# Splitting the query projection between two layers into two halves, and a new order of the kept heads

## The chip, the cores and the metric

The kernel runs on one core of a Trainium2 chip. The metric is the device time of one launch in microseconds (us). Three runs of the kernel before took 1135.45, 1135.97 and 1137.13 us, so the median is 1135.97 us. TensorE is called PE here (its weight loads PEld), VectorE DVE, ScalarE ACT, GpSimd POOL, and SyncE, which issues every transfer, SP.

## The reference, cut to what matters

Two identical layers follow each other. Each is an attention block over a key/value cache and then a small mixer MLP. There are 8 batch elements with one token each, 16 query heads on 8 key/value heads, 4096 cached positions, 256 numbers to a head, and a model width of 448.

```
q = (x @ wq).reshape(B, Sq, Hq, Dh)            # 448 x 4096
scores = einsum(q, k) * Dh ** -0.5             # k, v: 8 x 8 x 4096 x 256 each
p = softmax(scores);  o = einsum(p, v)
x = x + o.reshape(B, Sq, Hq * Dh) @ wo         # 4096 x 448
x = x + mixer(x)                               # layernorm, w1..w4, gelu
# and the same again with the same caches and weights
```

With one token the shifts of the mixer bring in zeros only, so its first half reduces to `x1 = x`, and what is left is a layernorm, `w3`, gelu and `w4`. Both layers read the same caches. The second layer needs a batch element's keys and values again, with a query that is known only when that element has gone through the first layer and its MLP.

## The kernel before, in words

**Units.** The work is a list of units, written out by hand around line 354. A unit (p, b, g) is layer p (1 or 2), batch element b, key/value head g. A unit has four steps, each with one tile of keys and one tile of values of 128 x 2048 bf16 numbers (512 KB). For a batch element come first the units of layer 1, then `GAP, lone..., GAP`, then the units of layer 2. A GAP is an empty unit. A lone unit belongs to another batch element; it gives the engines something to do while this element's attention output goes through `wo`, the MLP (`mid_steps`) and `wq`. Batch elements 0 to 3 have two lone units there, elements 4 to 7 one. This text calls the stretch from the last layer-1 unit to the first layer-2 unit of the element the passage, and the place where the layer-2 units begin the fence (the dict `fence`, line 372).

**Kept and loose heads.** Keys arrive raw, DVE transposes them (line 502), and `k_part` (line 590) multiplies them with the block-diagonal query `Qblk`. Heads 2 to 7 (`KEEP` = 6) keep their transposed keys in SBUF from layer 1 to layer 2, apart from two tiles that are parked in PSUM and copied back by ACT (line 474). Heads 0 and 1 are loose: their keys are loaded and transposed a second time. Values are always loaded twice (`v_part`, line 569).

**Slots.** There are 31 slots of 512 KB. Of those, 22 hold kept keys during a passage, so that everything else goes round in the other nine. `pump` (line 465) takes the next transfer of a fixed list and the slot that came free longest ago. SP issues the transfers in that order, one behind the other; each waits until the last reader of its slot is done, and at most eight are under way.

**Order of the values.** `plan` says at which step a value tile is used: six steps after its keys' step as a rule, earlier for the last head of layer 1. `late_v` makes an exception: the two loose layer-2 heads of the element before are scored between the kept heads of layer 2, but their values are held back to the next passage (these are the held heads; their probabilities lie in `pt_far`). Their eight value tiles were planned at steps 0, 1, 4, 5, 6, 7, 8 and 9 of the passage, the last head's own at steps 2, 2, 3 and 3.

**The dense steps.** `mid_steps` (line 256) is a generator. The main loop takes one piece of it per step through `dense_next`; what the pieces leave for DVE and ACT waits in `between` and is emitted at the next `flush`. Its last pieces are `variance` and the query projection: 16 groups of seven matmuls with `wq` (`in_mms`, lines 132 and 140), then one ACT multiplication `scaled` (line 340) that writes the query. When that is emitted, `make_blocks` may call `expand` for the first layer-2 units (PE line 155, ACT line 161). At the fence the loop runs whatever is left of the generator (line 735) before the first `k_part` of layer 2.

**PE is in order.** A matmul whose tile has not landed holds up all that follows on PE, the dense steps too.

Of the kernel before, what the change touches and what calls it, by code (L numbers as in the profile page):

```python
# [18 lines left out]
KEEP = 6  # L19
# [8 lines left out]
def kernel(  # L28
# [14 lines left out]
    nc = tc.nc  # L43

    Bn, Sq, D = A_x.shape
    G, S, Dh = A_k_cache.shape[1:]
# [4 lines left out]
    HJ = Hq * 2  # L51
# [16 lines left out]
    nr, xm, cc, hx, hu = (  # L68
        small[:, 21:23],
        small[:, 23:27],  # L70
        small[:, 27:31],
        small[:, 31:45],
        small[:, 45:59],
    )
# [3 lines left out]
    wq_sb = consts.tile([128, 3, HD], BF16, name="wq_sb")  # L78
    wq_tl = consts.tile([128, HD // 2], BF16, name="wq_tl")
# [110 lines left out]
    between = []  # L190

    def flush():
        while between:
            between.pop(0)()

    q_done = set()
# [54 lines left out]
    def bursts(n, k, spread):  # L251

        m = -(-n // k) if spread else n
        return [range(i, min(i + m, n)) for i in range(0, n, m)]

    def mid_steps(b, spread):

        xs = X[:, b, :]  # L260
        res = {}

        def first():
            nc.vector.tensor_tensor(out=xs, in0=xs, in1=y1[:, b, :], op=ALU.add)
            total(xs)

        between.append(first)
        yield
        norm_rows(xs, res)
        yield  # L270
        variance(TWICE)
        hT = work.tile([128, HC], BF16, tag="hT", bufs=1)
        hpf = room(HC)
        hp = hpf.rearrange("p (i m) -> p i m", i=2)
        for ms in bursts(HC // 2, 2, spread):
            in_mms(hp[:, :, ms[0] : ms[-1] + 1].unsqueeze(3), w3_sb, w3_tl, res["rows"], HC, ms)
            if ms[-1] + 1 < HC // 2:
                yield

        def gelu():  # L280
            nc.vector.tensor_scalar(
                out=hx, in0=hpf, scalar1=nr[:, 1:2], scalar2=None, op0=ALU.mult
            )
            nc.vector.scalar_tensor_tensor(
                out=hu, in0=hx, scalar=0.044715, in1=hx, op0=ALU.mult, op1=ALU.mult
            )
            nc.vector.scalar_tensor_tensor(
                out=hu, in0=hu, scalar=1.0, in1=hx, op0=ALU.add, op1=ALU.mult
            )
            nc.scalar.activation(hu, hu, ACT.Tanh, scale=0.7978845608028654)  # L290
            nc.vector.scalar_tensor_tensor(
                out=xs, in0=cc, scalar=nr[:, 0:1], in1=xs, op0=ALU.mult, op1=ALU.add
            )

            between.append(
                lambda: nc.vector.scalar_tensor_tensor(
                    out=hT[:], in0=hu, scalar=1.0, in1=hx, op0=ALU.add, op1=ALU.mult
                )
            )

        between.append(gelu)
        yield
        yield
        yp = room(4)
        for cs in bursts(4, 2, spread):
            for c in cs:
                for m in range(HC):
                    nc.tensor.matmul(  # L308
                        yp[:, c : c + 1],
                        chunk(w4_sb[:, m, :], c),  # L310
                        hT[:, m : m + 1],
                        start=(m == 0),
                        stop=(m == HC - 1),
                    )
            if cs[-1] < 3:
                yield

        def more():
            nc.vector.scalar_tensor_tensor(
                out=xs, in0=yp, scalar=0.5, in1=xs, op0=ALU.mult, op1=ALU.add  # L320
            )
            total(xs)

        between.append(more)
        yield
        norm_rows(xs, res)
        yield

        variance(((256.0, 256.0 * EPS),))
        q2 = qT2[:, :, b % 2].rearrange("p (i m) -> p i m", i=2)  # L330
        qp = room(HJ).rearrange("p (i m) -> p i m", i=2)
        for ms in bursts(HJ // 2, 3 if spread else 2, True):
            in_mms(
                qp[:, :, ms[0] : ms[-1] + 1].unsqueeze(3), wq_sb, wq_tl, res["rows"], HJ, ms, True
            )
            if ms[-1] + 1 < HJ // 2:
                yield

        def scaled():
            nc.scalar.mul(q2, qp, nr[:, 0:1])  # L340
            q_done.add(b)

        between.append(scaled)

    heads = list(range(G))
    loose = heads[: G - KEEP]

    second = heads[G - KEEP // 2 :] + heads[G - KEEP : G - KEEP // 2]  # L350
    parked = {(second[-1], 4 - PARKED + i): i for i in range(PARKED)}
    GAP = None
    ahead = {b: [(2, b - 1, g) for g in loose] for b in range(1, Bn)}
# [3 lines left out]
    units = []  # L357
    ends = {}
    fence = {}
    late_v = {}  # L360
    half = KEEP // 2
    for b in range(Bn):
        if b:
            units += [(1, b, g) for g in heads[len(loose) :]]
        else:
            units += [(1, b, g) for g in heads[:-half]] + ahead[0] + [(1, b, g) for g in heads[-half:]]
        ends[len(units) - 1] = b
        at = 4 * len(units)
        ps = [(units.index(u), s) for u in ahead[b] for s in range(4)]
        late_v.update(zip(ps, [at + i for i in (0, 1, 4, 5, 6, 7, 8, 9)]))  # L370
        units += [GAP] + lone[b] + [GAP]
        fence[len(units)] = b
        units += [(2, b, g) for g in second[:half]] + ahead.get(b + 1, []) + [(2, b, g) for g in second[half:]]
# [13 lines left out]
    t = 0  # L387
# [127 lines left out]
    def dense_next():  # L515
        flush()
        if dense and next(dense[0], "end") == "end":
            dense.pop(0)
# [3 lines left out]
    def make_blocks(t):  # L522

        if t in runs and t not in ready:
            p, b, g = units[t]
            if p == 1 or b in q_done:
                x, n = runs[t]
                qT = qT1[:, :, b] if p == 1 else qT2[:, :, b % 2]
                expand(Qblk[x], qT[:, 4 * g : 4 * (g + n)], n, scb[t % 2])
                ready.add(t)  # L530
# [49 lines left out]
    def k_part(t, s):  # L580
        u = units[t]
        p, b, g = u
        if s == 0:
            scs[t] = scb[t % 2][:, 0:64].rearrange("p (c b h) -> p c b h", b=4, h=2)
        key = (u if fresh(u, s) else (1, b, g)), s
        ktv = kt_of[key][:].rearrange("p (e c m x) -> p e c m x", e=4, c=2, x=2)
        for c in range(2):
            for db in range(4):
                for x in range(2):
                    nc.tensor.matmul(  # L590
                        scs[t][:, 2 * s + c, :, :],
                        ktv[:, db, c, :, x],
                        Qblk[run_of[t][0]][:, run_of[t][1], db, x, :, :],
                        start=(db == 0 and x == 0),
                        stop=(db == 3 and x == 1),
                    )
        if p == 2 or g in loose or (g, s) in parked:
            free.append(kt_of.pop(key))
            pump()
# [129 lines left out]
    for t in range(n_units + 1):  # L729
        cur = t < n_units  # L730
        for q in range(4):
            i = 4 * t + q
            if cur:
                if t in fence and q == 0:
                    while dense:
                        dense_next()
                    flush()
                    make_blocks(t)
                late = q == 0 and t and not beside[t]
                if beside[t]:  # L740
                    transposes(i)
                flush()
                if not late and not beside[t]:
                    transposes(i)
                if units[t]:
                    k_part(t, q)
            back = t and units[t - 1]
            if q == 0 and back:
                max_mms(t - 1)
                exps(t - 1)  # L750
            if cur and late:
                transposes(i)
            if back and q == 1:
                to_rows(t - 1)
                sums(t - 1)
            if q == 2 and not cur:
                mark(t - 2)
            for u, s in plan.get(i, []):
                v_part(u, s)
                if s == 3:  # L760
                    head_out(u)
            if q == 3 and cur and t > 1 and t - 2 not in ends:
                mark(t - 2)
            if q == 3 and t - 1 in ends:
                mark(t - 1)
            dense_next()
            if q > 1:
                make_blocks(t + 1)
            if cur and units[t] and q == 3:
                max_reduce(t)  # L770
# [112 lines left out]
```

## Time and profile before

The profiled execution took 1135.04 us, of which its span is 1133.0 us; that is 0.93 us under the median of the three runs.

| what | value |
|---|---|
| span | 1133.0 us |
| DMA moved | 449.83 MB, mean 397 GB/s |
| PE busy / PEld busy | 62% / 57% of the span |
| DVE / ACT / POOL busy | 49% / 27% / 9% |
| chain that ended last: transfers | 66% |
| transfers of 512 KB | 512 of values, 320 of keys |
| median from issue to landing | 9.9 us |

The page's second part cuts the span in 40 equal slices of 28.3 us and gives the busy tenths of each engine and the rate of the transfers in each. The chain of part 4 is followed back from the last instruction to whatever released each step. "Issue" in it is time in which an engine waited for nothing that the profile shows. Further views used are a table of busy times by stretch, the timeline of a stretch, and the list of what SP waited for.

### The profile page before, as it was taken

The page shows a single profiled execution, that of the slowest core. Times are in us where ns is not written, and L with a number is a line of the kernel's source. Part 1 is how long each engine was busy: PE and PEld are TensorE (multiplying, and loading weights), DVE is VectorE, ACT ScalarE, POOL GpSimd, SP SyncE. Part 2 cuts the span into 40 slices and gives each one's busy share as a digit, 9 for nine tenths or more (in the row PEclk, how much of TensorE's full clock was granted, in tenths as well). Part 3 has the DMA queues.
Part 4 walks back from the last instruction along what each step waited for, and adds up shares of the span by engine and source line. Part 5 has one row for each costly group of instructions (what it writes and reads, how often), then busy time and mean ns, then how long its engine had stood idle before and what let it go on. Part 6 is the DMA issues. An engine that isn't in the chain of part 4 may idle for free.

```text
span 1133.0 us, 47063 instructions
## 1 busy us (share of the span) xinstructions
PE 700.0 (62%) x20769; PEld 641.9 (57%) x20769; DVE 554.9 (49%) x1305; ACT 308.1 (27%) x1384; POOL 104.4 (9%) x156
## 2 busy tenths in 40 slices
PE   3155666666766576665666666655666666665765
PEld 3144565555655466555655556655656565655665
DVE  5267445544464445643556434643456435643332
ACT  2022124221342213321243212422143213421241
POOL 0000001000010000100010000000010000100001
DMA  9999999999999999999999999999999999999991
GB/s 361 386 417 418 413 391 415 417 416 399 416 416 417 407 392 413 417 417 400 406 415 417 417 396 358 417 416 417 363 400 417 416 411 372 416 417 417 372 415 77
DMA packets 127196, 449.83 MB, mean 397 GB/s; under 512 B 13568, under 2 KB 19600, under 8 KB 126608
## 3 DMA queue, kind: packets, MB, share of 16 engines
q1 hardware_dynamic: 126992, 446.83, 98.5%
q8 instruction: 162, 2.65, 0.8%
q14 instruction: 42, 0.34, 0.1%
HBM read 446.77 MB, written 0.01 MB: 394 GB/s over the span
## 4 chain that ended last, share of the span: by engine, by line
DMA 66%; PE 16%; DVE 6%; issue 5%; ACT 4%; SPq 2%; POOL 0%; POOLq 0%; DVEq 0%; ACTq 0%
DMA slot<-in_A_v_cache_dram 43%; DMA slot<-in_A_k_cache_dram 22%; PE bank L569 5%; DVE slot L502 4%; PE bank L590 3%; PE bank L132 2%; SPq L478 2%; ACT pt L657 1%; PE bank L613 1%; PE bank L177 1%; DVE small L623 1%; ACT pe L626 1%; PE bank L308 1%; PE bank L649 1%; ACT slot L474 1%
## 5 line engine op out<-in xcount | busy, mean ns | idle before, releaser
L502 DVE STREAM_TRANSPOSE slot<-slot 128x512 f32<-128x512 f32 x640 | 414.6, 688 | 215.9 <-DMA slot<-in_A_k_cache_dram 142.4
L569 PEld LDWEIGHTS <-slot 128*128 128x128 bf16 x8192 | 268.9, 105 | 335.0 <-DMA slot<-in_A_v_cache_dram 300.8
L569 PE MATMUL bank<-pt,slot 128*128 128x2 bf16 x7168 | 260.8, 166 | 269.0 <-DMA slot<-in_A_v_cache_dram 237.4
L590 PE MATMUL bank<-Qblk,slot 128*128 128x8 bf16 x8192 | 294.4, 168 | 41.6 <-issue 19.5
L590 PEld LDWEIGHTS <-slot 128*128 128x128 bf16 x8192 | 266.6, 105 | 49.0 <-issue 33.2
L626 ACT ACTIVATE pe<-bank,small 128x32 bf16<-128x32 f32 x256 | 61.7, 297 | 435.1 <-DVE small L623 435.0
L668 POOL TENSOR_TENSOR small<-small 128x2 f32<-128x2 f32 x112 | 78.4, 700 | 779.6 <-DVE small L664 779.6
L657 ACT CAST pt<-bank 32x64 bf16<-32x64 f32 x448 | 91.1, 203 | 108.1 <-PE bank L649 103.7
L623 DVE TENSOR_REDUCE small<-bank 128x2 f32<-128x256 f32 x128 | 54.1, 422 | 116.4 <-PE bank L613 116.1
L664 DVE TENSOR_REDUCE small<-bank 128x2 f32<-128x64 f32 x128 | 28.1, 220 | 141.4 <-ACT pt L657 91.3
L161 ACT CAST Qblk<-bank 32x32 bf16<-32x32 f32 (+1 forms) x304 | 53.0, 174 | 81.8 <-PE bank L155 78.0
L613 PE MATMUL bank<-rows,small 128*128 128x128 bf16 x256 | 48.6, 293 | 18.9 <-DVE small L605 18.8
L569 PE MATMUL bank<-pt_far,slot 128*128 128x2 bf16 x1024 | 37.6, 166 | 25.1 <-DMA slot<-in_A_v_cache_dram 22.6
L649 PE MATMUL bank<-pe,rows 128*128 128x64 bf16 x512 | 51.3, 241 | 1.9 <-issue 1.9
L649 PEld LDWEIGHTS <-rows 128*128 128x128 bf16 x512 | 33.8, 124 | 29.3 <-issue 29.3
L639 PE MATMUL bank<-pe,small 128*128 128x64 bf16 x128 | 27.3, 213 | 28.8 <-ACT pe L626 27.6
L605 DVE TENSOR_REDUCE small<-bank 128x2 bf16<-128x64 f32 x128 | 25.5, 199 | 35.4 <-PE bank L590 35.0
L177 PEld LDWEIGHTS <-wo_sb 128*128 128x128 bf16 x1152 | 35.4, 104 | 7.3 <-issue 7.3
L538 ACT ACTIVATE OT<-bank,small 128x2 bf16<-128x2 f32 x122 | 25.6, 261 | 48.0 <-PE bank L569 47.2
L132 PEld LDWEIGHTS <-wq_sb 128*128 128x128 bf16 x864 | 30.1, 106 | 13.2 <-issue 8.7
L474 ACT COPY slot<-park 128x1024 bf16<-128x1024 bf16 x32 | 31.0, 1027 | 23.7 <-DVE slot L502 23.7
L177 PE MATMUL bank<-OT,wo_sb 128*128 128x1 bf16 x1024 | 33.1, 165 | 4.5 <-ACT OT L538 4.5
(113 smaller groups left out, 386.6 us busy)
## 6 DMA issues: line engine op xcount, KB each, us to landing
slot<-in_A_v_cache_dram SPq DMA_DIRECT2D x512, 512.0 KB, 9.9
slot<-in_A_k_cache_dram SPq DMA_DIRECT2D x320, 512.0 KB, 9.9
wo_sb<-in_A_wo_dram SPq DMA_DIRECT2D x4, 896.0 KB, 9.2
wq_sb<-in_A_wq_dram SPq DMA_DIRECT2D x3, 1024.0 KB, 6.9
w_sb<-in_B_w_dram SPq DMA_DIRECT2D x1, 1568.0 KB
w_sb<-in_B_w_dram SPq DMA_DIRECT2D x3, 448.0 KB, 10.1
wq_tl<-in_A_wq_dram SPq DMA_DIRECT2D x2, 256.0 KB, 10.1
w_tl<-in_B_w_dram SPq DMA_DIRECT2D x2, 112.0 KB, 9.3
```

The source lines that it names most:

```text
L132: nc.tensor.matmul(pv[:, i, j, :], cols(big[:, c, :], m + i * half), rows[:, c, :], start=(i == 0 and j == 0 and c == 0), stop=True, skip_ ...
L161: nc.scalar.copy(dst, src)
L177: nc.tensor.matmul(y[:, c, :], chunk(wo_sb[:, k, :], c), o[:, k, :], start=False, stop=True, skip_group_check=True,)
L502: nc.vector.transpose(dst[:, q], src[:, q])
L569: nc.tensor.matmul(pos[t][:, k, :], vv[:, c, 128 * k : 128 * k + 128], pts[t][:, 8 * s + c, :], start=(t == 0 and s == 0 and c == 0 and k ...
L590: nc.tensor.matmul(scs[t][:, 2 * s + c, :, :], ktv[:, db, c, :, x], Qblk[run_of[t][0]][:, run_of[t][1], db, x, :, :], start=(db == 0 and x ...
L613: nc.tensor.matmul(mzs[t][:, 128 * h : 128 * h + 128], pm[:, h : h + 1].to_broadcast([128, 128]), ident, start=True, stop=True,)
L623: nc.vector.tensor_reduce(nm, mx, AX.X, ALU.max, negate=True)
L626: nc.scalar.activation(pe[:].rearrange("p c b h -> p h (c b)")[:, h], scs[t].rearrange("p c b h -> p h (c b)")[:, h], ACT.Exp, bias=nm[:, ...
L649: nc.tensor.matmul(pp[:, c], sel, pe[:], start=True, stop=True)
L657: nc.scalar.copy(pts[t][sl].rearrange("p (k c) h -> p k c h", c=4), pp[sl, :, :, pb, :].rearrange("p c k h -> p k c h"),)
L668: nc.gpsimd.tensor_tensor(out=rz_of[t], in0=zs, in1=mone, op=ALU.pow)
```

## The change

1. The 16 groups of the query projection are cut in two. Part 1 (groups 8 to 15: heads 2, 3, 6 and 7) comes first, with its own `scaled`; then the generator passes two steps, and part 0 (groups 0 to 7: heads 0, 1, 4 and 5) follows in two pieces of four groups. `q_done` holds (element, part), and `make_blocks` asks for the part that its run of heads needs.
2. At the fence only part 1 has to be done. What is left of part 0 is taken by the following `dense_next` calls, beside the kept heads.
3. The layer-2 order of an element becomes 2, 3, 6, 7, then the loose 0, 1, then 4, 5 (before: 5, 6, 7, then 0, 1, then 2, 3, 4). For the last element, whose loose heads stand at the end, it is 2, 3, 6, 7, 4, 5, 0, 1. The two parked tiles are now those of head 5 and not of head 4.
4. The held heads' eight value tiles are planned at steps 4, 4, 5, 5, 6, 7, 8 and 9 of the passage, so that the first two stand behind the last layer-1 head's own values, in the list of transfers and on PE.

```diff
-        for ms in bursts(HJ // 2, 3 if spread else 2, True):
-            in_mms(
-                qp[:, :, ms[0] : ms[-1] + 1].unsqueeze(3), wq_sb, wq_tl, res["rows"], HJ, ms, True
-            )
-            if ms[-1] + 1 < HJ // 2:
+        for part in (1, 0):
+            for k in range(2 if spread or not part else 1):
+                n = 4 if spread or not part else 8
+                ms = range(8 * part + n * k, 8 * part + n * k + n)
+                in_mms(
+                    qp[:, :, ms[0] : ms[-1] + 1].unsqueeze(3),
...
+                if ms[-1] % 8 < 7:
+                    yield
+
+            def scaled(part=part):
+                sl = slice(8 * part, 8 * part + 8)
+                nc.scalar.mul(q2[:, :, sl], qp[:, :, sl], nr[:, 0:1])
+                q_done.add((b, part))
+
+            between.append(scaled)
+            if part:
                 yield
-
-        def scaled():
-            nc.scalar.mul(q2, qp, nr[:, 0:1])
-            q_done.add(b)
-
-        between.append(scaled)
+                yield
...
-    second = heads[G - KEEP // 2 :] + heads[G - KEEP : G - KEEP // 2]
+    second = [2, 3, 6, 7, 4, 5]
...
-    half = KEEP // 2
+    half = 4
...
-            units += [(1, b, g) for g in heads[:-half]] + ahead[0] + [(1, b, g) for g in heads[-half:]]
+            units += [(1, b, g) for g in heads[:5]] + ahead[0] + [(1, b, g) for g in heads[5:]]
...
-        late_v.update(zip(ps, [at + i for i in (0, 1, 4, 5, 6, 7, 8, 9)]))
+        late_v.update(zip(ps, [at + i for i in (4, 4, 5, 5, 6, 7, 8, 9)]))
...
-            if p == 1 or b in q_done:
+            if p == 1 or (b, g % 4 // 2) in q_done:
...
-                    while dense:
-                        dense_next()
+                    flush()
+                    while (fence[t], 1) not in q_done:
+                        next(dense[0])
+                        flush()
                     flush()
                     make_blocks(t)
```

More of the change, by code (lines that the diff above doesn't have):

```diff
@@ L331, in mid_steps @@
         qp = room(HJ).rearrange("p (i m) -> p i m", i=2)
-        for ms in bursts(HJ // 2, 3 if spread else 2, True):
-            in_mms(
-                qp[:, :, ms[0] : ms[-1] + 1].unsqueeze(3), wq_sb, wq_tl, res["rows"], HJ, ms, True
-            )
-            if ms[-1] + 1 < HJ // 2:
+        for part in (1, 0):
[4 more added lines that the diff above has]
+                    qp[:, :, ms[0] : ms[-1] + 1].unsqueeze(3),
+                    wq_sb,
+                    wq_tl,
+                    res["rows"],
+                    HJ,
+                    ms,
+                    True,
+                )
+                if ms[-1] % 8 < 7:
[6 more added lines that the diff above has]
+            if part:
                 yield
-        def scaled():
-            nc.scalar.mul(q2, qp, nr[:, 0:1])
-            q_done.add(b)
-        between.append(scaled)
+                yield
     heads = list(range(G))
     loose = heads[: G - KEEP]
-    second = heads[G - KEEP // 2 :] + heads[G - KEEP : G - KEEP // 2]
+    second = [2, 3, 6, 7, 4, 5]
     parked = {(second[-1], 4 - PARKED + i): i for i in range(PARKED)}
@@ L583, in k_part @@
         if s == 0:
+            assert t not in runs or t in ready
             scs[t] = scb[t % 2][:, 0:64].rearrange("p (c b h) -> p c b h", b=4, h=2)
```

## The prediction

> **What bounds the kernel now.** First the slices: what do the transfers do over the span?
>
> ```profile
> DMA  9999999999999999999999999999999999999991
> GB/s 361 386 417 418 413 391 415 417 416 399 416 416 417 407 392 413 417 417 400 406 415 417 417 396 358 417 416 417 363 400 417 416 411 372 416 417 417 372 415 77
> q8 instruction: 162, 2.65, 0.8%
> ```
>
> Most slices stand at 416 to 418 GB/s, so the transfers are the bound, one of 512 KB (524,288 bytes) taking 524,288 / 417,000 = 1.26 us. What can be won is where the rate dips, once for each of the eight passages. The table of stretches says how much:
>
> ```profile
> 388.00:408.00 20.00, 12.67 (x362) 11.50 (x359) 7.83 (x27) 3.48 (x17) 1.39 (x2) 1.00 1.01 371
> 292.00:308.00 16.00, 10.38 (x318) 9.77 (x316) 10.60 (x21) 4.52 (x23) 1.40 (x2) 1.00 1.03 416
> 688.00:704.00 16.00, 11.00 (x329) 10.18 (x329) 11.43 (x23) 4.81 (x24) 1.40 (x2) 1.00 0.91 327
> 808.00:824.00 16.00, 9.30 (x301) 8.94 (x299) 7.18 (x14) 3.25 (x17) 1.10 (x2) 1.00 0.84 300
> 936.00:952.00 16.00, 9.10 (x277) 8.60 (x278) 8.82 (x17) 3.77 (x21) 0.70 (x1) 1.00 0.91 339
> 1060.00:1076.00 16.00, 10.34 (x325) 9.83 (x321) 5.09 (x11) 4.13 (x21) 0.71 (x1) 1.00 0.92 340
> ```
>
> The last number is GB/s. Length times (1 - rate/417) is the time missing: behind the fences of the four late passages (elements 4 to 7, one lone unit) 3.5, 4.5, 3.0 and 2.9 us, together 13.9 us. The early passages (elements 0 to 3) lose nothing behind the fence (292 to 308: 416 GB/s) except element 0 (158 to 174: 383 GB/s, 1.3 us); they lose some earlier, 2.2 us in 388 to 408. Why does the first late passage starve? Its timeline:
>
> ```profile
> 665.24 0.59 PE L569 MATMUL bank<-pt,slot 128*128 128x2 bf16 x16 [0.68 <-DMA slot<-in_A_v_cache_dram]
> 666.39 0.99 PE L177 MATMUL bank<-OT,wo_sb 128*128 128x1 bf16 x32 [0.56 <-ACT OT L538]
> 670.30 0.59 PE L233 MATMUL bank<-small 128*128 128x1 f32 x2 [0.75 <-DVE small L224]
> 674.43 1.64 PE L308 MATMUL bank<-hT,w_sb 128*128 128x1 bf16 x56 [0.29 <-DVE hT L296]
> 685.04 0.32 PE L132 MATMUL bank<-small,wq_sb 128*128 128x1 bf16 x6 [1.99 <-issue]
> 686.04 0.30 ACT L340 ACTIVATE qT<-bank,small 128x32 bf16<-128x32 f32 x1 [6.06 <-PE bank L140]
> 686.63 0.18 PEld L155 LDWEIGHTS <-rows 128*128 128x128 bf16 x4
> 687.92 1.85 PE L590 MATMUL bank<-Qblk,slot 128*128 128x8 bf16 x64 [1.02 <-ACT Qblk L161]
> 688.32 3.83 DVE L502 STREAM_TRANSPOSE slot<-slot 128x512 f32<-128x512 f32 x6 [6.68 <-PE bank L590]
> ```
>
> SP's waits from 684 to 704 (what it waited for: us, times, longest):
>
> ```profile
> SPq L478 <- DVE slot L502: 4.8, 3, 3.7
> SPq L478 <- PE bank L569: 4.0, 2, 3.6
> ```
>
> The last value tile of layer 1 starts at 665.24, as it lands; then wo, the MLP and wq run as one chain to the first kept head at 687.92. Only that head gives back a kept slot, DVE transposes into it, and only then are there slots for loads. SP waits for these transposes and for value tiles used late in the passage. So each us by which the late fences come sooner is up to a us of transfers, until what is missing is used up.
>
> **The change part by part.**
>
> *Held values behind the last head's.* Layer 1's last values land two transfers sooner, 2 x 1.26 = 2.5 us, and wo with them. But PE now meets all eight held tiles in order behind wo, not six. By the list of transfers (last value tile, two held tiles, a key tile, two held tiles) the fourth lands five transfers, 6.3 us, after the last value tile; the first `variance` (670.30), planned behind it, came 5.1 us after that tile's start until now and would come at 6.3 + 0.5 = 6.8 us, which takes back 1.7 of the 2.5. Next late are the third and fourth lone key tiles, whose places in the list are the same as before: the fourth's transposes (now 670.30 to 671.61) stay where they are. So the MLP is about 0.7 us sooner. Ends: 0 (a transfer later) and 2.5 us (nothing waits).
>
> *wq in halves, late passages.* A group takes 0.19 us (eight from 679.81 to 681.30). Today from `variance` (679.36) to the fence (687.92) it is 8.56 us, 1.99 of them the pause marked "issue". After it: 0.24 to wq, eight groups 1.49, two lone value tiles 0.85, a wait of 0.6 for the smaller `scaled` (DVE, POOL 0.55, ACT 0.3 behind the last group), the expand 0.15, two value tiles 0.85, four groups 0.75: 4.9 us. The 1.02 us in which PE waits for ACT's copies of `Qblk` is then covered by value tiles and groups; were that cover gone, it would come back whole. So 8.56 - 1.99 - 4.9 = 1.6 us sooner, with the 0.7 us 2.3 us at the first key tile. Behind it four more groups stand between that tile and the next: the second to fourth key tiles come only 2.3 - 0.75 = 1.5 us sooner. The new `scaled` is one ACT instruction of 0.3 us beside those tiles.
>
> *The pause.* Each late passage has one of 1.99, 2.37, 2.37 and 2.36 us before the fence. 20,769 matmuls and as many weight loads over 162 packets of q8 are 256 to a packet, so a packet is a block of PE's program. Counted in the built order, the block ends that carry these pauses stand 129, 93, 65 and 29 instructions before the first key tile; after the change 39 before it, then 5, 41 and 85 behind its start. So three of the four pauses move behind that first tile, which would then come up to 2.3 + 2.3 = 4.6 us sooner, while the tiles after it keep the 1.5 us. The Trainium skill's page "Runtime: NRT & Kernel Launch", section "Instruction fetch mechanics", says that the program is streamed in blocks of 256 instructions and that crossing one is mostly hidden: the count agrees, the 2 us of "issue" in these passages do not. By that rule the pause would fall away on both sides and the sum below would be the same.
>
> *What the transfers get.* The first load behind the fence waits for the second transpose after the first key tile, the next for the second key tile's slot, in SP's one queue. So the gain per passage lies between 1.5 us (second tile) and 4.6 (first tile), and at most what is missing. I take 2.3, the first key tile without the pause, nearest to what the head of the queue waits for: three passages give 6.9. After the last fence the chain goes on through PE with pauses of "issue" (1082, 1087, 1093, 1105, 1111 us), so PE's instructions count: 66 fewer of 41,555 rows (by the built order) at 256 in 5.9 us (PE resumes from two such block ends at 679.1 and 685.0) are 1.5 us. Sum: 6.9 + 1.5 = 8.4 us. Ends: 4 x 1.5 = 6.0, and 13.9.
>
> *Early passages.* There the generator has 13 steps and ends before the fence in both kernels: the pieces of wq only move among steps, and the two tiles more on PE (2 x 0.58 us) meet a start 2.5 us sooner. Behind these fences nothing is missing, so 0. Ends: a gain of 1.3 (element 0), and a loss of one transfer in each, 5.0, if slots come late before the fence, where 371 GB/s shows that they are already short.
>
> *Order of heads.* Each unit frees four key tiles in either order, so slots in use are equal step by step; pairs 2-3, 6-7, 0-1, 4-5 need four expands for five (0.25 PE and 0.75 ACT each), beside transfers: 0. The parked tiles' second transposes (2.6 us of DVE) come a head later; DVE is at 49%: 0, and a loss of one transfer per element, 10 us, if that holds up a slot. SP issues the same 832 loads; POOL does nothing new.
>
> **The rivals.** (a) *Held tiles hold up the chain* (slower). PE waits in order for the fourth held tile. If slots reach it three transfers later, `variance` comes at 6.8 + 3.8 = 10.6 us after the last value tile, 3.1 us later than now in absolute time; less the 1.6 of wq, 1.5 us lost in each of four late passages, 6.0 us, 1142. It decides from two transfers on (1.8 us later, 1.6 back). For it: nine slots go round, and SP's waits name value tiles. Against: these loads' slots come from the last head's values, which are used sooner too. (b) *The pause eats it* (same). If pauses behind the first key tile delay the second to fourth by what was won, and SP's queue stands on those, the late passages give 0 to 0.5 us each: 1135. For it: three block ends fall there. Against: one load and two transposes come before. (c) *All that is missing is won* (faster still): 13.9 us, 1122, if the head of the queue follows the first tile alone.
>
> **How the numbers follow.** The profiled execution's own 1135.04 us less 8.4 is 1126.6; it was 0.93 under the median, so 1127.6. Chances: forecast (gains of 3 to 11 us) 0.64, (c) 0.11, (b) 0.10, (a) or the transfer-per-element losses of the parked tiles 0.15. Under 0.2% (2.3 us) a measurement cannot tell from no change. So faster 0.75, same 0.10, slower 0.15. The range leaves out the far half of (c) and most of (a): 1122 to 1138. The forecast alone: 1124 to 1133.
>
> **What the profile would show.** Right: in the late passages wo 2.5 us sooner against the transfers, an idle time before a held tile "<-DMA" behind it, eight groups of wq, a shorter "Qblk" wait at the first kept tile, four groups between it and the next, and 350 to 400 GB/s in the four stretches. Wrong: stretches as before with the fence sooner (SP waits for something else), or a fence no sooner (held tiles, pause). A rate under 410 anywhere between passages would mean the new order costs slots.

## The result, and the profile after

The changed kernel takes 1127.99 us (median of four runs, 1126.38 to 1129.67); the kernel before, on the same chip, 1136.14 us (1135.45 to 1137.13). The ratio is 0.9928, with an interval of 0.9911 to 0.9945: 8.15 us faster, where 8.4 was forecast. The profiled execution of after is the longest of its four, 1129.67 us, so the two profiles differ by only 1135.04 - 1129.67 = 5.4 us. What is read from them below is where the time went, not how much it was.

The page of after, its slices and its line for the instruction stream:

```profile
DMA  9999999999999999999999999999999999999991
GB/s 362 387 418 418 409 405 409 418 416 386 416 417 417 407 396 416 416 417 389 406 416 417 417 395 403 417 417 411 372 402 417 417 415 400 415 417 410 391 416 65
q8 instruction: 162, 2.65, 0.8%
```

The transfers are still the bound, and the four deep dips of before (358, 363, 372, 372) have become 403, 372, 400 and 391. The table of stretches shows the same places, shifted by what was won before each (columns: stretch and length, then busy time of PE, PEld, DVE, ACT and POOL, granted clock, DMA share, GB/s):

```profile
292.00:308.00 16.00, 9.27 (x287) 8.82 (x283) 10.38 (x20) 3.94 (x19) 1.40 (x2) 1.00 1.03 416
684.00:700.00 16.00, 10.62 (x333) 10.16 (x334) 9.95 (x20) 4.01 (x19) 1.40 (x2) 1.00 1.02 399
808.00:824.00 16.00, 10.30 (x322) 9.74 (x320) 9.04 (x18) 4.51 (x22) 0.82 (x2) 1.00 0.97 359
932.00:948.00 16.00, 10.95 (x342) 10.43 (x340) 9.47 (x19) 5.43 (x26) 1.00 (x3) 1.00 1.02 386
1058.00:1074.00 16.00, 9.36 (x293) 8.94 (x291) 6.15 (x14) 6.21 (x22) 1.40 (x2) 1.00 1.02 387
```

The first row belongs to an early passage, where nothing was missing and nothing is; the other four lie behind the late fences. They stood at 327, 300, 339 and 340 GB/s. How the first late passage now runs (timeline; the brackets are idle time ahead of a row and what ended it):

```profile
664.11 0.58 PE L582 MATMUL bank<-pt,slot 128*128 128x2 bf16 x16 [0.66 <-DMA slot<-in_A_v_cache_dram]
665.26 0.99 PE L177 MATMUL bank<-OT,wo_sb 128*128 128x1 bf16 x32 [0.56 <-ACT OT L551]
...
669.16 0.58 PE L582 MATMUL bank<-pt_far,slot 128*128 128x2 bf16 x16 [0.73 <-DMA slot<-in_A_v_cache_dram]
670.40 0.59 PE L582 MATMUL bank<-pt_far,slot 128*128 128x2 bf16 x16 [0.66 <-DMA slot<-in_A_v_cache_dram]
670.85 0.57 PE L233 MATMUL bank<-small 128*128 128x1 f32 x2
...
682.12 0.25 PE L155 MATMUL bank<-qT,rows 128*128 128x8 bf16 x4 [0.41 <-ACT qT L350]
682.23 0.99 PE L582 MATMUL bank<-pt,slot 128*128 128x2 bf16 x32
...
685.24 0.26 PE L132 MATMUL bank<-small,wq_sb 128*128 128x1 bf16 x4 [1.78 <-issue]
...
685.77 0.57 PE L604 MATMUL bank<-Qblk,slot 128*128 128x8 bf16 x16
...
686.94 1.21 PE L604 MATMUL bank<-Qblk,slot 128*128 128x8 bf16 x40
```

The first row is the last value tile of layer 1, the two `pt_far` rows are held tiles for which PE now waits, L233 at 670.85 is the first `variance`, L155 the expand, and the two L604 rows are the first two kept key tiles. From the first row to the first kept tile it is 685.77 - 664.11 = 21.66 us, against 687.92 - 665.24 = 22.68 before, although that first row now stands two transfers earlier in the list. The wait for `Qblk` ahead of the first kept tile (1.02 us before) is gone.

**Where the transfers were short, in one measure.** For every kernel below, the same two stretches are cut at each late passage: "ahead", from 8 us before to 16 us after the start of layer 1's last value tile, and "behind", the 26 us that follow and hold the fence. Length times (1 - rate / 417) is the time missing, as in the prediction. These are the rows for after:

```profile
656.00:680.00 24.00, 16.36 (x478) 15.70 (x479) 8.89 (x36) 5.14 (x25) 1.56 (x3) 1.00 1.00 388
680.00:706.00 26.00, 17.36 (x550) 16.33 (x547) 13.01 (x27) 7.15 (x34) 2.91 (x5) 1.00 1.02 405
780.00:804.00 24.00, 15.34 (x448) 14.69 (x449) 8.28 (x34) 4.29 (x21) 1.39 (x2) 1.00 1.00 386
804.00:830.00 26.00, 17.62 (x544) 16.57 (x545) 12.59 (x26) 6.75 (x33) 2.65 (x4) 1.00 0.99 378
905.00:929.00 24.00, 16.29 (x469) 15.55 (x470) 8.43 (x35) 5.13 (x25) 1.39 (x2) 1.00 1.03 415
929.00:955.00 26.00, 17.32 (x552) 16.54 (x550) 13.76 (x28) 7.26 (x35) 3.35 (x5) 1.00 1.02 397
1028.00:1052.00 24.00, 15.75 (x449) 15.02 (x450) 8.19 (x34) 4.51 (x22) 1.39 (x2) 1.00 1.01 402
1052.00:1078.00 26.00, 17.88 (x580) 17.23 (x580) 7.68 (x18) 11.10 (x39) 2.65 (x4) 1.00 1.02 395
```

and these the two rows of before to which 780 and 1028 answer:

```profile
784.00:808.00 24.00, 16.58 (x492) 15.78 (x493) 8.08 (x34) 4.32 (x22) 2.25 (x4) 1.00 1.02 415
1035.00:1059.00 24.00, 16.34 (x478) 15.50 (x479) 8.02 (x34) 4.51 (x23) 2.10 (x3) 1.00 1.03 415
```

Summed over the four late passages, in us, with the measured gain beside it (difference of medians to the kernel before in the same comparison):

| kernel | missing behind | missing ahead | both | gain in time |
|---|---|---|---|---|
| before | 14.7 | 2.1 | 16.8 | |
| order alone | 13.5 | 3.6 | 17.2 | 0.1 |
| held values alone, early passages | 16.3 | 2.5 | 18.8 | 0.3 |
| held values alone, late passages | 11.6 | 2.6 | 14.2 | 5.9 |
| held values alone, all passages | 11.7 | 2.1 | 13.8 | 5.5 |
| halves and order, without held values | 7.9 | 5.2 | 13.0 | 5.5 |
| after, held values late only | 6.1 | 4.0 | 10.1 | 7.0 |
| after | 5.8 | 4.4 | 10.2 | 8.2 |
| after, again (`e0_after`, `e11_after_again`) | 4.3, 5.4 | 5.2, 3.7 | 9.5, 9.1 | 8.6, 8.8 |
| after, pauses moved | 3.7 | 5.4 | 9.1 | 8.8 |
| after, part 0 later | 2.4 | 6.1 | 8.5 | 8.4 |
| after, both of these | 2.4 | 5.8 | 8.3 | 9.3 |
| after, part 0 left out | 1.9 | 5.9 | 7.9 | 9.6 |

The stretches come from one execution each, the gains from four to fifteen, with an interval of 1.0 to 1.9 us to either side, so the columns need not agree to a microsecond or two (the third row misses 2.0 us more than before and takes the same time; this execution of before also misses 1.3 us behind element 0's fence, of which the others miss 0.0 to 1.0). Two things stand out: behind the fences after won 14.7 - 5.8 = 8.9 us, and ahead of them it lost 4.4 - 2.1 = 2.3 us that before did not lose, mostly in the second and the fourth late passage (386 and 402 GB/s where before had 415).

### The profile page after: what moved, and what is told of

Its sections match the earlier page's. It is cut to its first block, busy times and chain, and to the rows that moved or that the text cites. A ratio compares the mean times of both kernels' runs of the same rounds, so it can differ in the third digit from the quotient of the medians.

```text
span 1127.9 us, 46955 instructions
## 1 busy us (share of the span) xinstructions
PE 698.8 (62%) x20737; PEld 641.7 (57%) x20737; DVE 555.2 (49%) x1305; ACT 306.6 (27%) x1360; POOL 104.1 (9%) x156
## 4 chain that ended last, share of the span: by engine, by line
DMA 67%; PE 14%; issue 6%; DVE 6%; ACT 4%; SPq 2%; POOL 1%; DVEq 0%; POOLq 0%; ACTq 0%
DMA slot<-in_A_v_cache_dram 41%; DMA slot<-in_A_k_cache_dram 26%; PE bank L582 4%; DVE slot L515 4%; PE bank L604 3%; SPq L491 2%; PE bank L132 2%; ACT pt L671 2%; PE bank L627 1%; ACT pe L640 1%; DVE small L637 1%; PE bank L177 1%; PE bank L663 1%; PE bank L308 1%; PE bank L653 1%
## 5 line engine op out<-in xcount | busy, mean ns | idle before, releaser
L604 PE MATMUL bank<-Qblk,slot 128*128 128x8 bf16 x8192 | 293.5, 168 | 41.1 <-issue 20.8
L604 PEld LDWEIGHTS <-slot 128*128 128x128 bf16 x8192 | 265.3, 105 | 48.2 <-issue 30.1
L678 DVE TENSOR_REDUCE small<-bank 128x2 f32<-128x64 f32 x128 | 28.1, 220 | 123.6 <-ACT pt L671 100.6
L161 ACT CAST Qblk<-bank 32x32 bf16<-32x32 f32 (+1 forms) x272 | 48.3, 178 | 86.5 <-PE bank L155 83.7
L132 PE MATMUL bank<-small,wq_sb 128*128 128x1 bf16 x768 | 28.1, 165 | 6.0 <-issue 5.8
## 6 DMA issues: line engine op xcount, KB each, us to landing
w_sb<-in_B_w_dram SPq DMA_DIRECT2D x3, 448.0 KB, 10.1
wq_tl<-in_A_wq_dram SPq DMA_DIRECT2D x2, 256.0 KB, 10.2
```

Of the source, the lines that this page charges most:

```text
L132: nc.tensor.matmul(pv[:, i, j, :], cols(big[:, c, :], m + i * half), rows[:, c, :], start=(i == 0 and j == 0 and c == 0), stop=True, skip_ ...
L161: nc.scalar.copy(dst, src)
L604: nc.tensor.matmul(scs[t][:, 2 * s + c, :, :], ktv[:, db, c, :, x], Qblk[run_of[t][0]][:, run_of[t][1], db, x, :, :], start=(db == 0 and x ...
```

## The experiments

**The change once more, as a control for the first comparison** (`e0_after`, no edit).

> The changed kernel once more, beside the three that follow. Every theory expects it 7 to 9 us under the kernel before (first measurement: 1127.99 against 1136.14, and single runs of it lay 3.3 us apart).

1127.87 us against 1136.51, ratio 0.9922 (0.9908 to 0.9935): the first result holds, and the parts below are measured against the same runs of before.

**Halves and order, without the held values.**

```diff
-        late_v.update(zip(ps, [at + i for i in (4, 4, 5, 5, 6, 7, 8, 9)]))
+        late_v.update(zip(ps, [at + i for i in (0, 1, 4, 5, 6, 7, 8, 9)]))
```

> wq in halves and the new order of heads, but the held heads' values planned at steps 0, 1, 4, 5, 6, 7, 8, 9 as before. My theory (the late fences come 1.6 us sooner by the halves and 0.7 us by the held values): 6 us less than before, 1130. Theory that the held values do it all: as before, 1136. Theory that the order of heads does it: 1128, as the whole change.

1131.01 us (1129.36 to 1133.14), ratio 0.9951 (0.9938 to 0.9963): 5.5 us, 1.4 per late passage. From the last value tile of layer 1 to the first kept tile it is 21.1, 18.6, 18.7 and 20.6 us against 22.7, 22.7, 21.9 and 23.1 before, and to the second kept tile 22.3, 21.7, 21.9 and 23.4 against 23.1, 23.2, 22.3 and 23.5. So the first tile comes 2.9 us sooner on average, the second 0.7, and what was gained lies between.

**Held values alone**, on the kernel before.

```diff
-        late_v.update(zip(ps, [at + i for i in (0, 1, 4, 5, 6, 7, 8, 9)]))
+        late_v.update(zip(ps, [at + i for i in (4, 4, 5, 5, 6, 7, 8, 9)]))
```

> The kernel before with only the held heads' values moved behind the last head's (steps 4, 4, 5, 5, 6, 7, 8, 9). My theory: 0.7 us in each of four late passages less some 0.4 us lost in each early passage, 1 to 2 us under before, 1134.5. Theory that the held values do it all: 1128. Theory that the order does it: 1136.

1130.97 us (1130.11 to 1133.29), ratio 0.9955 (0.9942 to 0.9969): 5.5 us as well. That is twice the 4 x 0.7 = 2.8 us of the prediction, and the 1 to 2 us expected here were missed by more.

**The order of the heads alone**, on the kernel before.

```diff
-    second = heads[G - KEEP // 2 :] + heads[G - KEEP : G - KEEP // 2]
+    second = [2, 3, 6, 7, 4, 5]
...
-    half = KEEP // 2
+    half = 4
...
-            units += [(1, b, g) for g in heads[:-half]] + ahead[0] + [(1, b, g) for g in heads[-half:]]
+            units += [(1, b, g) for g in heads[:5]] + ahead[0] + [(1, b, g) for g in heads[5:]]
```

> The kernel before with only the order of the layer-2 heads changed to 2, 3, 6, 7, 0, 1, 4, 5 (parked tiles of head 5); wq whole, held values as before. My theory: no difference, 1136 (within 1.5 us). Theory that the order of heads does it: 1128 to 1130.

1136.40 us against 1136.51, ratio 1.0000 (0.9991 to 1.0008): nothing, to within 1 us. The parked tiles' later second transposes cost no slot that counts.

**Held values moved only in the late passages**, once in after and once on the kernel before; and only in the early ones, on the kernel before. The edit that the first makes in after:

```diff
-        late_v.update(zip(ps, [at + i for i in (4, 4, 5, 5, 6, 7, 8, 9)]))
+        late_v.update(
+            zip(ps, [at + i for i in ((4, 4) if b >= 4 else (0, 1)) + ((5, 5) if b >= 4 else (4, 5)) + (6, 7, 8, 9)])
+        )
```

> The changed kernel, but the held values stand behind the last head's only in the four late passages; in the four early ones they are planned as before. My prediction counted the early passages at nothing: then as the changed kernel, 1128. If moving them also gains in the early passages (the move alone gained 5.5 us, twice what I had priced for the late ones): 1129.5 to 1131.

1128.65 us (1127.54 to 1129.18) against 1135.67, ratio 0.9938 (0.9926 to 0.9949): 7.0 us, which can't be told from after. The other two, on the kernel before, take `(4, 4, 5, 5)` in place of `(0, 1, 4, 5)` for b < 4 or for b >= 4 alone:

```diff
+            zip(ps, [at + i for i in ((4, 4, 5, 5) if b < 4 else (0, 1, 4, 5)) + (6, 7, 8, 9)])
```

> The kernel before, with the held values behind the last head's in the four early passages only. My prediction: nothing gained there, 1136, within 1.5 us. If the early passages are where the unexplained part of the held values' gain (5.5 measured, 2.8 priced) comes from: 2 to 3 us less, 1133 to 1134.

1136.78 us against 1137.08, ratio 0.9996 (0.9987 to 1.0005): nothing. So the early passages' share is 0, as forecast.

```diff
+            zip(ps, [at + i for i in ((4, 4, 5, 5) if b >= 4 else (0, 1, 4, 5)) + (6, 7, 8, 9)])
```

> The kernel before, with the held values behind the last head's in the four late passages only. By my 0.7 us for each passage: 2.8 us less, 1133. If a late passage gives more than I priced, up to the whole start of 2.5 us: 5 us less or more, 1131 or below, and then the early passages give nothing.

1131.23 us (1130.04 to 1132.05), ratio 0.9948 (0.9935 to 0.9962): 5.9 us, 1.46 per late passage. All of what the held values give is here. The last late passage in this kernel's timeline (L571 is its `v_part`, L592 its `k_part`):

```profile
1036.65 0.58 PE L571 MATMUL bank<-pt,slot 128*128 128x2 bf16 x16 [0.72 <-DMA slot<-in_A_v_cache_dram]
...
1041.63 0.59 PE L571 MATMUL bank<-pt_far,slot 128*128 128x2 bf16 x16 [0.67 <-DMA slot<-in_A_v_cache_dram]
1042.88 0.59 PE L571 MATMUL bank<-pt_far,slot 128*128 128x2 bf16 x16 [0.66 <-DMA slot<-in_A_v_cache_dram]
1043.33 0.56 PE L233 MATMUL bank<-small 128*128 128x1 f32 x2
...
1060.68 0.42 PE L571 MATMUL bank<-pt,slot 128*128 128x2 bf16 x10 [2.36 <-issue]
...
1062.23 0.92 PE L592 MATMUL bank<-Qblk,slot 128*128 128x8 bf16 x29 [1.02 <-ACT Qblk L161]
```

The two waits for held tiles and the first `variance` 1043.33 - 1036.65 = 6.7 us after the last value tile are there as the prediction has them. From the last value tile (1036.65) to the first kept tile (1062.23) the passage takes 25.6 us, 2.5 more than before; the first three late passages take 0.7, 0.3 and 2.8 more. With a start 2.5 us sooner that leaves 1.9, 2.2, -0.3 and 0 us, 0.9 on average, which is near the 0.7 of the prediction and below the 1.46 that the medians give. The stretches show 2.6 us won in the late passages (16.8 to 14.2). The rest of the 5.9 us was not found in the profiles, which themselves differ by only 1135.04 - 1130.94 = 4.1 us.

**The pauses moved.** After, with 48 small matmuls more at the start of the program (96 PE instructions), so that every block end of 256 instructions stands 96 instructions earlier in the work.

```diff
+    for _ in range(48):
+        nc.tensor.matmul(dnb[:, 0:1], identb, identb[:, 0:1], start=True, stop=True)
```

> The changed kernel with 96 PE instructions more (48 matmuls of one column that nobody reads) at the start, while PE waits for wq. They move every end of a 256-instruction block: in the late passages the ends stand 135, 91, 55 and 11 instructions before the first kept tile, and none is left between the first and the second (before the shift: 39 before, then 5, 41, 85 behind). If the pauses belong to the block ends, the idle time of about 2 us marked issue moves before the first kept tile in all four, and the second kept tile follows 1.2 us behind the first. Time: if SP's queue stands on the first kept tile, 2 to 6 us slower (1130 to 1134); if it stands on the second and later ones, the same or up to 2 us faster (1126 to 1128).

1126.89 us (1125.96 to 1128.40) against 1135.67, ratio 0.9925 (0.9912 to 0.9938): 8.8 us, as after. The pauses did move. The last late passage of after has its longest pause between the first and the second kept tile, and two shorter ones ahead of both:

```profile
1048.89 0.64 PE L308 MATMUL bank<-hT,w_sb 128*128 128x1 bf16 x18 [0.36 <-issue]
...
1054.83 0.72 PE L582 MATMUL bank<-pt,slot 128*128 128x2 bf16 x21 [0.89 <-issue]
...
1057.11 0.57 PE L604 MATMUL bank<-Qblk,slot 128*128 128x8 bf16 x16
...
1060.77 0.19 PE L140 MATMUL bank<-small,wq_tl 128*128 128x2 bf16 x1 [2.37 <-issue]
1060.81 1.34 PE L604 MATMUL bank<-Qblk,slot 128*128 128x8 bf16 x45
```

With the shift the long one lies ahead of both:

```profile
1056.94 0.27 PE L132 MATMUL bank<-small,wq_sb 128*128 128x1 bf16 x4 [1.83 <-issue]
...
1057.10 0.57 PE L604 MATMUL bank<-Qblk,slot 128*128 128x8 bf16 x16
...
1058.27 1.85 PE L604 MATMUL bank<-Qblk,slot 128*128 128x8 bf16 x64
```

The second tile follows the first by 1.17 us instead of 3.70. In that passage 0.4 us is missing behind the fence instead of 1.4, but 1.8 ahead of it instead of 0.9. Over all passages no change of the time can be told. But the pauses did not stay 2 us long where they went: ahead of the first kept tile they are now 0.93, 1.37, 1.08 and 1.83 us, and that tile comes 21.5, 21.2, 21.6 and 22.1 us after the last value tile, where after has 21.7, 21.5, 21.5 and 21.2. So the first tile did not come 2 us later, and this run does not show what a later first tile would cost. It brought the second tile 1.5 us sooner on average, and that gave nothing that the time shows.

**Part 0 later.** In the late passages the second half waits four steps more, so that the first kept tiles follow each other without groups between them.

```diff
             if part:
                 yield
                 yield
+                for _ in range(0 if spread else 4):
+                    yield
```

> The changed kernel, but in the late passages part 0 of wq starts four steps later, so that all eight of its groups come behind the fourth tile of the first kept head and none before the first or between the first and second. The first kept tile comes 0.75 us sooner, the second 1.5 us. If the queue stands on these tiles: 2 to 5 us faster (1123 to 1126). If the missing time is used up or the pauses decide: 1127 to 1129.

1127.24 us (1124.72 to 1130.63), ratio 0.9927 (0.9912 to 0.9942): 8.4 us, no better than after. The tiles do follow each other: in three of the four late passages the second comes 0.43 us behind the first. In the second late passage the first kept tile (L606 in this kernel) directly follows the last lone value tiles (L584), with no group of wq and no pause between:

```profile
805.64 0.25 PE L155 MATMUL bank<-qT,rows 128*128 128x8 bf16 x4 [0.40 <-ACT qT L350]
805.75 0.99 PE L584 MATMUL bank<-pt,slot 128*128 128x2 bf16 x32
806.73 0.97 PE L606 MATMUL bank<-Qblk,slot 128*128 128x8 bf16 x31
```

This takes what is missing behind the fences down to 2.4 us, from 5.8 in after; ahead of them it is up from 4.4 to 6.1.

**Both of these together** (the two edits above).

> The changed kernel with part 0 of wq four steps later in the late passages and the 96 PE instructions at the start, both together. If each gives what its single run hinted at (0 to 1 us, within the spread): 1125 to 1127. If the transfers are now held by something else, as the change without part 0 suggests (1 us at most): as the changed kernel, 1127 to 1128.

1127.74 us (1127.53 to 1128.36) against 1137.08, ratio 0.9918 (0.9905 to 0.9932). The control of that comparison, after itself:

> The changed kernel itself, beside these, so that the combined version is compared with it on the same chip. Every theory: 8 to 9 us under the kernel before, 1127 to 1128.

1128.33 us (1125.92 to 1129.59), ratio 0.9920 (0.9906 to 0.9934). There is no difference to tell between the two. Here are the four stretches ahead of the late fences, and the four behind them, in the kernel with both edits:

```profile
656.00:680.00 24.00, 15.12 (x434) 14.39 (x434) 7.68 (x32) 4.44 (x22) 1.39 (x2) 1.00 0.99 391
680.00:706.00 26.00, 18.57 (x599) 17.86 (x598) 13.78 (x29) 7.85 (x39) 3.34 (x5) 1.00 1.02 405
779.00:803.00 24.00, 16.19 (x471) 15.53 (x472) 9.10 (x36) 5.06 (x25) 1.39 (x2) 1.00 1.02 404
803.00:829.00 26.00, 17.65 (x568) 16.76 (x566) 12.95 (x27) 7.20 (x35) 3.02 (x5) 1.00 1.02 410
902.00:926.00 24.00, 16.32 (x464) 15.51 (x465) 8.77 (x36) 5.25 (x25) 1.55 (x3) 1.00 1.01 393
926.00:952.00 26.00, 17.85 (x564) 16.63 (x561) 12.92 (x27) 7.13 (x34) 2.87 (x5) 1.00 1.02 400
1028.00:1052.00 24.00, 15.92 (x464) 15.01 (x463) 7.82 (x33) 4.66 (x23) 2.09 (x3) 1.00 0.99 379
1052.00:1078.00 26.00, 17.31 (x562) 16.55 (x559) 7.46 (x17) 10.20 (x36) 1.95 (x3) 1.00 1.03 414
```

The rows behind are at 400 to 414, close to full; those ahead are at 379 to 404, where before had 410 to 415 in the last three. What the two edits win behind the fences, 5.8 - 2.4 = 3.4 us, is given back in part, 5.8 - 4.4 = 1.4 us, ahead of them.

**Part 0 left out.** In the late passages the second half of the projection is not computed; heads 0, 1, 4 and 5 of layer 2 take the queries of 2, 3, 6 and 7.

```diff
                 q_done.add((b, part))
+                if b >= 4 and part:
+                    nc.scalar.mul(q2[:, :, 0:8], qp[:, :, 8:16], nr[:, 0:1])
+                    q_done.add((b, 0))
...
                 yield
                 yield
+                if b >= 4:
+                    break
```

> The changed kernel, leaving out part 0 of wq in the late passages (heads 0, 1, 4 and 5 of layer 2 get the queries of 2, 3, 6 and 7 there). It measures what the second half costs where it now stands, a bound for any other place. If it is hidden beside the kept heads: 1127 to 1129. If its groups and the block end that they bring forward hold up the kept heads: 1123 to 1126.

1126.11 us (1123.59 to 1126.24) against 1135.67, ratio 0.9910 (0.9897 to 0.9924): 9.6 us. The first fence's stretch is full:

```profile
684.00:700.00 16.00, 10.30 (x314) 9.57 (x315) 10.69 (x21) 3.73 (x18) 1.40 (x2) 1.00 1.03 418
```

So the second half, where the change puts it, costs about 1 us in all (9.6 us of gain against 8.2 to 8.8 of after, with intervals that reach down to nothing), much less than the 4 x 1.5 = 6 us that its eight groups keep PE busy.

## Why the prediction was right, point by point

**The sum.** 8.4 us forecast, 8.15 measured (8.6 and 8.8 when repeated); 1127.6 against 1127.99 us. That the two lie within 0.3 us is in part luck: both terms of the sum, 2.3 us for each of three passages and 1.5 for the last, do not hold as they were worked out (below), and the parts measured alone do not add up to it. The direction and the place hold. Rivals (a), slower by held tiles, and (b), eaten by the pause, are out; rival (c), 13.9 us, was not reached, not even without part 0.

**Where it lies: right.** The four late passages carry it. Behind their fences after wins 3.2, 2.1, 1.8 and 1.8 us by its profile, where 2.3, 2.3, 2.3 and 1.5 were set, and the four stretches stand at 359 to 399 GB/s (350 to 400 forecast). Set against the loss ahead of them, the four keep 3.0, 0.5, 2.1 and 1.0 us. In the early passages the held values measure nothing (0.3 us, interval from -0.6 to 1.5), and so does the order alone; the halves were not tried there apart, but the early stretches miss as much in after (8.2 us) as in before (7.8).

**Held values: the mechanism right, the size not settled.** The first `variance` comes 670.85 - 664.11 = 6.7 us after the last value tile (6.8 forecast), after waits of 0.73 and 0.66 us for held tiles; in the other late passages of after it comes 8.2, 6.7 and 7.2 us after it, so a held tile can be later than the list of transfers says (PE waits 2.20 us for one in the second late passage). The term was 0.7 us per late passage. The first kept tile comes 0.9 us sooner per passage by the one profile of the late passages alone, and the time falls by 1.46 us per passage, with an interval from 1.1 to 1.85. By the time this term was set too low; it lay between the ends given, 0 and 2.5.

**wq in halves: right in size.** By the prediction's working the first tile comes 1.6 us sooner, up to 2.3 more where the pause moves behind it, and the second 1.6 - 0.75 = 0.85. Measured alone it was 2.9 for the first and 0.7 for the second, and 1.4 per passage in the time. In after's timeline the new wait ahead of the expand is 0.41 us (0.6 forecast), the `Qblk` wait is gone, four groups stand ahead of the first kept tile and four between it and the second.

**What the transfers get: the traces point to the second kept tile, and the term was taken from the first.** The prediction took 2.3 us, the first key tile without the pause, out of a range from 1.5 (second tile) to 4.6 (first). In the last passage the traces tell the two apart. In before the first kept tile starts at 1065.73 and the second 0.43 us behind it, in one row:

```profile
1065.73 2.28 PE L590 MATMUL bank<-Qblk,slot 128*128 128x8 bf16 x80 [1.01 <-ACT Qblk L161]
```

In after they start at 1057.11 and 1060.81. From the second tile to the end of the span it takes 66.9 us in before and 67.1 in after, and 66.2 to 67.1 in the profiles of all kernels in which part 0 is neither put off nor left out; from the first tile it takes 67.3 in before and 70.8 in after. From the second tile to the next passage's last value tile of layer 1 it takes 103.3, 103.5 and 102.0 us in before and 100.8, 100.0 and 98.7 in after, where that value tile stands two transfers, 2.5 us, sooner in the list.

On average the second tile comes 24.3 us after the last value tile in after and 23.0 in before; with the start 2.5 us sooner that is 1.2 us won per passage (1.5 and 1.6 in the two repeats), close to the 1.5 of the prediction for the second tile. The first tile comes 3.7 us sooner, and the later work does not follow it. By this reading the choice of the tile was wrong, and by the second tile the sum would have been the prediction's lower end, 6.0 us.

Four passages at the second tile give 2.8 us for the halves with the order, 3.7 for the held values in the late passages and 5.0 for after, where the profiles lie 4.0, 4.1 and 5.4 us under that of before; the medians give 5.5, 5.9 and 8.2, and that rest was not found in the traces. The reading rests on these distances and holds up to after: the run with the pauses moved brought the second tile alone 1.5 us sooner, the distance stayed in three of the four passages (100.6 and 100.2 us to the next value tile, 66.8 to the end) and grew to 102.9 in the third, and the time shows nothing. Rival (b) named this tile, but the pauses did not eat what was won.

The 1.5 us of the last passage do not hold as worked out either. The 66 rows are nearly all one expand fewer for each of the eight elements (304 matmuls of L155 in before, 272 in after), and behind the last fence only one is left out (16 matmuls and 12), which is 8 rows, or 0.2 us at the prediction's own rate. The stretch from the second kept tile to the end is no shorter in after. What the last passage gained, 1.2 us by the same count, came ahead of that tile.

**The pause: counted right, and without a cost that the time shows.** One block end ahead of the first kept tile in the first late passage and three behind it in the others, with 1.78, 2.09, 1.82 and 2.37 us, as counted. Shifting them changes the time by nothing that can be told, and so does taking the groups away from between the tiles. That they belong to the instruction stream the trace shows directly: each of the 22 stops of after marked "issue" from 660 us on ends 2.2 to 2.4 us after a packet of q8 has started (in the last late passage packets start at 1046.55, 1052.53 and 1058.43 us, and PE resumes at 1048.89, 1054.83 and 1060.77). The rule of the Trainium skill's page "Runtime: NRT & Kernel Launch", section "Instruction fetch mechanics", that crossing a block of 256 instructions is mostly hidden, does not fit PE's idle time here (1.78 to 2.37 us each); for the time of this kernel it makes the same forecast as the count did.

**The steps as a sum: the point at which the working falls short.** The parts measured alone give 5.5 + 5.5 to 5.9 = 11.0 to 11.4 us, and together 8.15 to 8.8. With some 1.5 us of uncertainty on each, that is suggestive and no more; at the second kept tile the parts do add up (0.7 and 0.9 us per passage alone, 1.2 to 1.6 together). But the stretches show a loss that the prediction did not have: ahead of the late fences, 4.4 us missing for 2.1. By its own test ("a rate under 410 anywhere between passages would mean the new order costs slots") this would speak for a cost of the order, which it put at 0; but the order alone cost no time. Which part opens this dip is not settled. In the kernels without the new order (before, and held values alone, early or late) the last three late passages miss at most 0.4 us each ahead of the fence; in those with it they miss between 0.0 and 2.2. With the order alone only one passage shows it (1.4 us), and the time does not change; with the halves too, most do. Halves without the new order were not tried: the two halves are cut along that order.

**Rival (c), and why what is left cannot be had this way.** Behind the fences up to 14.7 - 1.9 = 12.8 of 14.7 us were won in the runs, so the head of SP's queue does come sooner with the fence. What SP waits for there is still DVE's transposes into the slots that the kept tiles give back, as in before (these waits of after, from 684 to 700: us in all, times, longest):

```profile
SPq L491 <- DVE slot L515: 4.8, 2, 2.7
SPq L491 <- DMA slot<-in_A_k_cache_dram: 3.4, 3, 1.8
```

But whatever more was won there, at most 1.5 us of it showed in the time, while the dip ahead of the next fences grew. In the three kernels that put part 0 off or leave it out, the second kept tile comes 3.1 to 3.5 us sooner still, but from it to the next passage's last value tile it takes 101.7 to 104.0 us, where after and its two repeats take 98.7 to 101.4: most of what is won at the tile is lost behind it. Whether the dip grows because less is missing behind the fence before it, or for a reason of the order, stays open; no run here separates them. The 1.4 us of the order alone stand behind a fence that still missed 4.8 us, which speaks for the order in that one passage.

## What to carry to other kernels

Where transfers bound a kernel and dip at a few places, price a change at those places alone: length times the missing share of the rate is the most that can be won there, and the parts' gains share it. When a late step is cured, measure the same stretches again and also the stretches ahead of them, since part of the gain may be lost in a place that had none to lose before. Measure each part of a change alone as well as the sum: here the sum was right to 0.3 us although its terms were not. Where two events could set the pace, measure from each of them to the next fixed point in every kernel: the one from which that distance stays the same is the one to price (here the second kept tile, 66.2 to 67.1 us ahead of the end).

## What the runs showed that was not expected

- PE stops where a block of 256 instructions of its program ends in dense work, for 0.36, 0.89 and 2.37 us at three block ends in a row in the last late passage of after, and each time it resumes 5.94 us after the resumption before. There the length of a stop is what the block's own work and its other waits leave of these 5.94 us. 96 instructions added at the start move the stops and change their lengths (0.93 to 1.83 us ahead of the first kept tiles), and the time shows no difference (8.8 us of gain against 8.2 to 8.8).
- A dip of the transfers at one place returned in part at another: with 12.3 us won behind the late fences (both edits), 3.7 us more were missing ahead of them.
